# Another written order for the first part of a delta-rule and feed-forward kernel, with eight more loads held behind TensorE

## The chip, the cores and the metric

The kernel runs on one core of a Trainium2 chip. A core has five engines, each working through its own list of instructions in order: TensorE (PE in the profile; its weight loads are shown apart as PEld), VectorE (DVE), ScalarE (ACT), GpSimd (POOL) and SyncE (SP), which here only issues transfers. Engines wait for each other, and for transfers, by semaphores. The metric is the device time of one execution in microseconds (us); less is better.

## What is computed

There are two blocks. The first is a delta-rule attention over 4 batches, 8 heads, 768 tokens and 48 channels: a 48x48 state for each batch and head is read by the query and corrected by the key at every token. The second takes its output, as 3072 rows of 384, through a feed-forward network with 2048 hidden units and the hard-swish function between its two matrix products.

```python
def _attn_ref(q, k, v, beta):
    k_n = k / (np.linalg.norm(k, axis=-1, keepdims=True) + 1e-06)
    ...
    for t in range(S):
        y[:, :, t] = einsum('bhd,bhde->bhe', q[:, :, t], state)
        v_old = einsum('bhde,bhd->bhe', state, kt)
        state = state + bt * einsum('bhd,bhe->bhde', kt, vt - v_old)

def _moe_ref(x, w_in, w_out):
    h = x @ w_in
    g = h * np.clip(h + 3.0, 0.0, 6.0) / 6.0
    return g @ w_out
```

The arrays q, k, v and beta arrive as 32-bit floats; both weight matrices arrive as 64-bit floats and are turned into 32-bit ones on the chip.

## The kernel before, in words

The 768 tokens are cut into 24 chunks t of 32 tokens; 4 batches x 32 tokens fill the 128 partitions. Within a chunk the recurrence becomes a triangular system. Its inverse is made for four chunks at a time on VectorE (`halves_of` for chunks 1 to 4, `inverse` for later ones); chunk 0 alone has its own way, a product of powers on TensorE (`product`). The feed-forward network works on blocks of two chunks.

For the first part of the run, every engine's order of work is written out by hand in the string ORDER. Each word is one step of a Python generator; `do` takes the words one after the other and emits the instructions of that step. `*n` repeats a word. The order in which an engine's instructions are emitted is the order in which it does them, so ORDER fixes all five lists at once. The words, with the generator's step counted from 0 behind a dot or, for loads, a number:

- k, q, v (`load_k`, L168; `load_q`, L180; `load_v`, L193): one load of 48 KB each, four of them (one for each batch) for each chunk; SP issues them. w (`load_w`, L331): one of 16 pieces of raw weights, 768 KB each, also on SP: w0 to w7 are of w_in, w8 to w15 of w_out. B (L1383): one of four loads of beta, issued by ScalarE. In this text k0 to k3 are the four loads of chunk 0's keys, w0 is the first piece of weights, and so on.
- a (`scales`, L356): one of four passes by ScalarE over the exponents of a piece of weights; c (`convert`, L378, L383, L389): one of three steps by VectorE that make 32-bit numbers of it. Piece i is made by a.4i to a.4i+3 and c.3i to c.3i+2; c.3i+2 needs a.4i+3.
- n0, n1, n2, n4 (`norms`): the keys' norms of chunk 0, chunk 1, chunks 2 and 3, chunk 4. For n0, n1, n4: .0 square on ScalarE (L407), .1 sum on VectorE (L413), .2 root on ScalarE (L417), .3 to .6 on VectorE (L420 to L431). n2 has two squares and two sums first.
- p0 to p4 (`prep`): .0 scales a chunk's keys on GpSimd (L510); .1 and .3 transpose keys and queries on TensorE (L524); .2 and .4 copy these to KQ on ScalarE (L532); .5 makes the products sc of keys and queries on TensorE (L547); .6 masks them on VectorE (L558). m (`mask`, L486) and b (`scaled`, L498) are GpSimd's parts of it.
- x0 (`product`): sixteen steps for chunk 0's inverse, by turns on VectorE (L606 to L656), TensorE (L596) and ScalarE (L624, L643).
- z (`settings`, VectorE): z.1 transposes beta to where all others read it (L255), which needs the four loads B; z.2 to z.5 are small constants. s (`more_settings`, GpSimd, L285 and L293): zeros in buffers.
- h0 (`chain` of chunk 0): .0 TensorE pz (L827), .1 ScalarE copy to R (L927), .2 TensorE su (L938), .3 VectorE state (L956). y0 is the rest of the chunk's output.
- i1 (`halves_of`): the inverse of chunks 1 to 4, which needs p1.6 to p4.6: i1.0 is the transpose A (L469), then some thirty small steps on VectorE (L730, L735), then the transpose X (L473); then x1 to x4 (`join`) finish it chunk by chunk on TensorE (L684).
- ua and ub, ra, ga and so on: pieces of the first matrix product (`up`, L994) for block 0, and their evaluation on ScalarE and VectorE; u: pieces of both matrix products for later blocks.

A capital K, Q, V or W is the same load with one more wait: `behind_tensor` makes its issue on SP wait until the last TensorE instruction emitted so far has ended. Before the change there is one such word, for w12.

The trace shows that the eighth load behind a piece of weights is issued only once that piece has landed: w0 is issued at 6.75 us and lands at 12.25, and the eighth load behind it, q4, is issued at 12.27. Where the loads go to buffers that are used again, they wait for the last reader too.

Of the kernel before, what the change touches and what calls it, by code (L numbers as in the profile page):

```python
# [19 lines left out]


ORDER = """
k*2 B*3 k*2 n0 k*2 z B s*2 n0*6 k*2 q*2 n1 q n1 q w k p0 z*3 k n1*2 k*2 n1*2 z p0*2 s k p0*3 a k a
m0 a n2 m1 p0 x0*2 w q x0 n1 x0*3 c*2 n2 a k s p1*2 a s*2 k q s*2 x0 n2 k*2 c x0 n2 x0 w q a*4 q p1
n2 k*2 a x0 m2 p1 c*2 p1 n2*3 b1 q b0 s p1 x0 q w x0 n2 q*2 c*3 x0 n4 k p1 k p2*2 x0*2 a*2 c a*2 q*3
a*2 w v p3*2 q x0 q n4 p2*2 c p2 v c n4*2 a*3 z v n4 c a m3 v c p2 n4*2 q p2 k c b2 h0 c h0 w a*2 h0
p4*2 a*2 m4 p3 q*4 h0 q k w p4*2 c*5 v*2 p3 k p3*3 k*2 p4*2 v*2 p4 m6 k a w a w i1*3 k i1*7 a i1*2 a
i1*2 v i1*2 k b3 k y0 c y0*3 ua*2 ra*2 i1*3 w v ga v a*3 i1*2 ua i1 h1 i1 q w ua ra ua i1 ra*2 ga i1
k ua a*2 ra ga i1 ga ua ra ua ra i1 ga i1*4 ua ga n5 x1*2 k x1 c a ra v a*2 ga x2 k*2 ga*2 ua*2 x1
ra*2 x1*2 ua h1*2 n5 k ga c ra ga*2 h1 c y1*2 ua ra w ga ua ra x2 n5 ga y1*2 ua ra ga h1 v*3 n5*2 k  # L30
y1*2 ua a ra x2 ub*2 a n5 rb*2 h1 x3 ga c*2 v W a h2 y2 gb ub rb gb x2 gb ub*2 n5*2 b4 rb n5 x2*2 h2
gb rb gb m5 a n5*2 ub rb gb v c q*2 v q*5 n5 ub n5 rb gb h2 y2 c h2 q ub y2*2 rb ub p5 b5 h2 rb gb*2
a*2 x3 p5 ub y2*2 k p5*2 h2 rb h3 p5 gb h3 ub*2 q rb gb rb gb ub a x3 p6 v c x4 x3 rb gb ub p7 rb gb
y3 c*2 v c p7*2 y3 v p7*2 b6 x3 q x3 ub h3 a p6*2 c p5*2 rb gb k m7 w p6 h3 u p6 k*2 q*3 a*2 y3 a p6
c y3 v y3*2 u n9 v k q a c a c*2 u*2 ru gu w k a*2 c a*2 x4 c*2 ru p7 a gu k u a*2 p7 p6 m8 u*3 a k
u*2 k h3 w ru*2 a*2 gu*2 x4 c*2 x4 k c*2 a p8 k a*2 u ru k h3 u*2 h4 ru a b8 gu k gu y4 p8*3 u h4
k*2 c q k*9 q u p8*2 k ru k*2 gu k c n9 q u q*2 p8 k*2 b7 n9*2 x4 i2 u x4 q i2*2 q ub ru gu u rb gb
i2*2 h4*2 u*2 i2 ru i2*6 y4 i2 gu i2*7 u i2 ru gu i2 u*3 ru i2*4 gu ru i2*2 v i2 c gu u*3 a u ru c
i2 u*2 i2 gu i2*3 q i2*5 y4 n9 i2 e*2 n9*2 i2*4 q i2 y4 e n9 u ru i2*3 u h4 i2 ru*2 gu h4 u n9 i2*2
u i2 e i2*6 y4 u k n9*3 u gu i2 y4 n9 i2 p9 q i2*2 gu  # L40
"""


# [1507 lines left out]
```

## Time and profile before

| what | value |
|---|---|
| median of three runs | 665.89 us (664.8 to 666.0) |
| the profiled execution's own time | 665.93 us |
| its span | 664.1 us |
| instructions in it | 26330 |
| TensorE matmul, busy | 636.2 us (96% of the span) |
| VectorE, busy | 487.1 us (73%) |
| ScalarE, busy | 272.1 us (41%) |
| GpSimd, busy | 203.5 us (31%) |
| moved by transfers | 33.27 MB, mean 50 GB/s |

The share of each engine is a mean over a short first part, in which the engines wait for one another, and a long second part, in which TensorE is busy nearly without a gap. The profile's slices and its table by stretches tell these parts from one another. In the timeline a row has the start, the length, the engine, the line and the operation with output and input; in square brackets stand the idle time just before it and what ended this. "SPq" rows are the issues of transfers by SP.

### The profile page before, as it was taken

To read this page: it belongs to the slowest core of one execution; us is meant where nothing else is said; L and a number is where in the kernel's file an instruction comes from. 1 tells how busy PE (TensorE), PEld (TensorE's weight loads), DVE (VectorE), ACT (ScalarE), POOL (GpSimd) and SP (SyncE) were. 2 spreads that over 40 slices of the span, in tenths; PEclk is the share of its full clock that TensorE was granted. 3 is DMA by queue.
4 is the path that set the end of the run, shared out by engine and by line. 5 is a ranking of instruction groups with operands and counts; after the bars stand their busy time and mean duration, and the time that the engine had idled before them with its cause. 6 is when DMAs were issued, how large, how long until landed. Compare 5 with 4: busy or idle time off the path is not lost.

```text
span 664.1 us, 26330 instructions
## 1 busy us (share of the span) xinstructions
PE 636.2 (96%) x11544; PEld 568.1 (86%) x11544; DVE 487.1 (73%) x1146; ACT 272.1 (41%) x532; POOL 203.5 (31%) x320
## 2 busy tenths in 40 slices
PE   2769999999999999999999999999999999999997
PEld 1658987776789989989989999999999999999997
DVE  4899867898555697657979748989658998456353
ACT  5897679331233143142144244244244144153350
POOL 6531112003511320562254354064052241331430
PEclk9659999999999999999999999999999999999999
DMA  7897246212140030041030030020020020000000
GB/s 175 206 236 197 76 98 161 49 28 41 23 83 8 10 66 3 2 85 27 2 74 3 2 74 3 3 61 2 3 50 2 2 50 1 23 19 2 25 1 25
DMA packets 88499, 33.27 MB, mean 50 GB/s; under 512 B 80160, under 2 KB 83232, under 8 KB 88384
## 3 DMA queue, kind: packets, MB, share of 16 engines
q1 hardware_dynamic: 88128, 31.29, 20.9%
q8 instruction: 91, 1.49, 0.9%
q10 hardware_dynamic: 256, 0.30, 0.2%
q14 instruction: 24, 0.20, 0.1%
HBM read 26.84 MB, written 4.72 MB: 48 GB/s over the span
## 4 chain that ended last, share of the span: by engine, by line
PE 90%; DVE 3%; DMA 2%; SPq 2%; ACT 1%; issue 1%; POOL 0%; ACTq 0%; DVEq 0%; POOLq 0%
PE po L1218 28%; PE ph L1066 20%; PE ph L994 16%; PE po L1154 6%; PE ks L806 3%; PE pt L524 3%; PE su L938 3%; PE pz L827 3%; PE py L827 3%; PE sc L547 3%; PE yt L873 1%; DMA spare<-in_moe_w_in_dram 1%; PE pi L684 1%; DMA w_out<-in_moe_w_in_dram 1%; SPq L168 1%
## 5 line engine op out<-in xcount | busy, mean ns | idle before, releaser
L1066 PE MATMUL ph<-xT,w_in 128*128 128x128 f32 (+1 forms) x560 | 121.4, 321 | 0.7 <-ACT KQ L532 0.5
L994 PE MATMUL ph<-xT,w_in 128*128 128x256 f32 (+1 forms) x576 | 117.1, 353 | 0.9 <-ACT xT L877 0.6
L1218 PE MATMUL po<-w_out,g 128*128 128x192 f32 x640 | 110.6, 326 | 0.0
L994 PEld LDWEIGHTS ph<-xT,w_in 128*128 128x128 f32 x576 | 95.2, 194 | 13.9 <-ACT xT L877 1.0
L1218 PEld LDWEIGHTS po<-w_out,g 128*128 128x128 f32 x640 | 104.6, 190 | 0.5
L1066 PEld LDWEIGHTS ph<-xT,w_in 128*128 128x128 f32 x560 | 91.1, 191 | 5.9 <-ACT KQ L532 0.7
L1030 POOL TENSOR_TENSOR g<-g 128x256 f32<-128x256 f32 x112 | 67.9, 608 | 83.2 <-ACT g L1080 78.8
L1218 PE MATMUL po<-spare,g 128*128 128x192 f32 x480 | 86.7, 332 | 0.0
L1218 PEld LDWEIGHTS po<-spare,g 128*128 128x128 f32 x480 | 77.2, 190 | 1.8
L1001 ACT ACTIVATE g<-ph,halves 128x256 f32<-128x256 f32 (+1 forms) x96 | 41.0, 436 | 74.2 <-PE ph L994 74.2
L1228 POOL TENSOR_TENSOR o<-o,u 128x192 f32<-128x192 f32 x18 | 13.2, 731 | 175.8 <-ACT o L1225 97.2
L1080 ACT ACTIVATE g<-ph 128x512 f32<-128x512 f32 x56 | 33.4, 597 | 81.8 <-PE ph L1066 81.8
L1204 DVE TENSOR_TENSOR g<-g 128x512 f32<-128x512 f32 x80 | 55.5, 715 | 5.6 <-PE po L1218 5.6
L759 DVE TENSOR_TENSOR pr<-A 128x30 f32<-128x30 f32 (+9 forms) x150 | 57.5, 383 | 2.7
L764 DVE TENSOR_TENSOR A<-A,pr 128x30 f32<-128x30 f32 (+9 forms) x150 | 55.7, 371 | 3.7
L1004 DVE SCALAR_TENSOR_TENSOR g<-g,ph 128x256 f32<-128x256 f32 (+1 forms) x96 | 34.7, 371 | 29.4 <-ACT g L1001 29.0
L356 ACT ACTIVATE spare<-spare,places 128x768 uint16<-128x768 uint16 (+1 forms) x56 | 52.6, 944 | 2.8 <-DMA kf<-in_k_dram 1.7
L1093 DVE TENSOR_TENSOR g<-ph,g 128x256 f32<-128x256 f32 x56 | 23.5, 420 | 38.5 <-PE ph L1066 30.9
L1225 ACT ACTIVATE o<-po 128x192 f32<-128x192 f32 x40 | 13.2, 330 | 83.2 <-PE po L1218 79.6
L1154 PE MATMUL po<-w_out,g 128*128 128x384 f32 x128 | 45.2, 491 | 0.0
L1107 DVE SCALAR_TENSOR_TENSOR g<-o,g 128x512 f32<-128x512 f32 x56 | 40.7, 726 | 5.9 <-ACT o L1104 5.9
L1104 ACT ACTIVATE o<-g,halves 128x512 f32<-128x512 f32 x56 | 40.4, 722 | 8.7 <-DVE g L1107 5.7
(141 smaller groups left out, 989.1 us busy)
## 6 DMA issues: line engine op xcount, KB each, us to landing
kf<-in_k_dram SPq DMA_DIRECT2D x96, 48.0 KB, 2.4
qb<-in_q_dram SPq DMA_DIRECT2D x96, 48.0 KB, 2.8
vf<-in_v_dram SPq DMA_DIRECT2D x96, 48.0 KB, 2.2
out_dram<-o SPq DMA_DIRECT2D x92, 48.0 KB, 1.6
spare<-in_moe_w_in_dram SPq DMA_DIRECT2D x4, 768.0 KB, 5.9
w_out<-in_moe_w_in_dram SPq DMA_DIRECT2D x4, 768.0 KB, 6.0
w_out<-in_moe_w_out_dram SPq DMA_DIRECT2D x4, 768.0 KB, 6.9
spare<-in_moe_w_out_dram SPq DMA_DIRECT2D x4, 768.0 KB, 5.0
```

The costliest lines, as they stand in the source:

```text
L356: nc.scalar.activation(out=z, in_=z if n else d.bitcast(I16)[:, :, :, 3], func=func, bias=places[:, n : n + 1], scale=scale,)
L759: nc.vector.tensor_tensor(out=pv, in0=A[:, j + 1 :, j].unsqueeze(2).to_broadcast([n, w, j]), in1=A[:, j, 0:j].unsqueeze(1).to_broadcast([n ...
L764: nc.vector.tensor_tensor(out=A[:, j + 1 :, 0:j], in0=A[:, j + 1 :, 0:j], in1=pv, op=ALU.subtract)
L994: nc.tensor.matmul(ph[:, cols], lhsT=w_in[:, s, f * 128 : (f + 1) * 128], rhs=xT[:, s, cols], start=(s == 0), stop=(s == NKT - 1),)
L1001: nc.scalar.activation(out=g, in_=ph, func=ACTF.Relu, bias=half, scale=1.0 / 6.0)
L1030: nc.gpsimd.tensor_tensor(out=out, in0=a, in1=b, op=op)
L1066: nc.tensor.matmul(ph[:, n], lhsT=w, rhs=x, start=start, stop=stop, skip_group_check=True)
L1104: nc.scalar.activation(out=r, in_=g, func=ACTF.Relu, bias=half, scale=1.0 / 6.0)
L1107: nc.vector.scalar_tensor_tensor(out=g, in0=r, scalar=1.0, in1=g, op0=ALU.min, op1=ALU.mult)
L1154: nc.tensor.matmul(pos[c][:], lhsT=gs[blk, f // 2][:, f % 2, c * P : (c + 1) * P], rhs=w_out[:, f, :], start=(f == 0), stop=(f == NFC - 1),)
L1204: nc.vector.tensor_tensor(out=A(f, *out, 4), in0=A(f, *a, 4), in1=A(f, *b, 4), op=op)
L1218: nc.tensor.matmul(ps[n][:], lhsT=A(f - f % 2, *a)[:, f % 2], rhs=b[:, f], start=(f == 0), stop=(f == HF - 1),)
```

## The change

Only the string ORDER changes; no function does. It has 782 words before and after. The 622 words that are not loads are the same words, in another order for about the first 120 of them (up to x0.15 and p2.6 in the list above, all well before i1.0); from there on their order is the same, but for two of GpSimd's s words that come later. The 156 loads that SP issues are the same too, but stand in other places over the whole of ORDER. Nine of them are held behind TensorE, where it was one: q11, v2, w6, w10, w11, k35, k37, w12 (as before) and w13.

The first SP loads before are k0 to k7, q0 to q3, w0, k8 to k13, w1; after, they are k0, k1, q0, k2 to k4, q1, q2, w0, k5, q3, k6 to k11, w1. On ScalarE, beta's third and fourth load were issued ahead of and behind n0.0, and are now both behind it. On VectorE, z.1 stood behind n0.6 and now stands ahead of it.

The diff:

```diff
 ORDER = """
-k*2 B*3 k*2 n0 k*2 z B s*2 n0*6 k*2 q*2 n1 q n1 q w k p0 z*3 k n1*2 k*2 n1*2 z p0*2 s k p0*3 a k a
-m0 a n2 m1 p0 x0*2 w q x0 n1 x0*3 c*2 n2 a k s p1*2 a s*2 k q s*2 x0 n2 k*2 c x0 n2 x0 w q a*4 q p1
-n2 k*2 a x0 m2 p1 c*2 p1 n2*3 b1 q b0 s p1 x0 q w x0 n2 q*2 c*3 x0 n4 k p1 k p2*2 x0*2 a*2 c a*2 q*3
-a*2 w v p3*2 q x0 q n4 p2*2 c p2 v c n4*2 a*3 z v n4 c a m3 v c p2 n4*2 q p2 k c b2 h0 c h0 w a*2 h0
-p4*2 a*2 m4 p3 q*4 h0 q k w p4*2 c*5 v*2 p3 k p3*3 k*2 p4*2 v*2 p4 m6 k a w a w i1*3 k i1*7 a i1*2 a
-i1*2 v i1*2 k b3 k y0 c y0*3 ua*2 ra*2 i1*3 w v ga v a*3 i1*2 ua i1 h1 i1 q w ua ra ua i1 ra*2 ga i1
-k ua a*2 ra ga i1 ga ua ra ua ra i1 ga i1*4 ua ga n5 x1*2 k x1 c a ra v a*2 ga x2 k*2 ga*2 ua*2 x1
-ra*2 x1*2 ua h1*2 n5 k ga c ra ga*2 h1 c y1*2 ua ra w ga ua ra x2 n5 ga y1*2 ua ra ga h1 v*3 n5*2 k
-y1*2 ua a ra x2 ub*2 a n5 rb*2 h1 x3 ga c*2 v W a h2 y2 gb ub rb gb x2 gb ub*2 n5*2 b4 rb n5 x2*2 h2
-gb rb gb m5 a n5*2 ub rb gb v c q*2 v q*5 n5 ub n5 rb gb h2 y2 c h2 q ub y2*2 rb ub p5 b5 h2 rb gb*2
-a*2 x3 p5 ub y2*2 k p5*2 h2 rb h3 p5 gb h3 ub*2 q rb gb rb gb ub a x3 p6 v c x4 x3 rb gb ub p7 rb gb
-y3 c*2 v c p7*2 y3 v p7*2 b6 x3 q x3 ub h3 a p6*2 c p5*2 rb gb k m7 w p6 h3 u p6 k*2 q*3 a*2 y3 a p6
-c y3 v y3*2 u n9 v k q a c a c*2 u*2 ru gu w k a*2 c a*2 x4 c*2 ru p7 a gu k u a*2 p7 p6 m8 u*3 a k
-u*2 k h3 w ru*2 a*2 gu*2 x4 c*2 x4 k c*2 a p8 k a*2 u ru k h3 u*2 h4 ru a b8 gu k gu y4 p8*3 u h4
-k*2 c q k*9 q u p8*2 k ru k*2 gu k c n9 q u q*2 p8 k*2 b7 n9*2 x4 i2 u x4 q i2*2 q ub ru gu u rb gb
-i2*2 h4*2 u*2 i2 ru i2*6 y4 i2 gu i2*7 u i2 ru gu i2 u*3 ru i2*4 gu ru i2*2 v i2 c gu u*3 a u ru c
-i2 u*2 i2 gu i2*3 q i2*5 y4 n9 i2 e*2 n9*2 i2*4 q i2 y4 e n9 u ru i2*3 u h4 i2 ru*2 gu h4 u n9 i2*2
-u i2 e i2*6 y4 u k n9*3 u gu i2 y4 n9 i2 p9 q i2*2 gu
+k*2 q B k s B k*2 z n0 q*2 B*2 n0 w k n0 q n0 s k n0*2 k*4 z k n1 n0 z p0*2 n1 p0 c w z k*2 n1 q z
+p0 q p0 a k m0 n1 q k q n1 a s a n1 w n2 s n1 p0 c a p0 x0 k x0 p1 q p1 x0*2 p1 s k n2 m2 n2 x0 b0 k
+x0 v a b1 k*2 n2*2 p1 x0 c x0 c*2 a*2 k p1 x0 a x0 n4 n2 w q s k a*2 c n2*3 a p1 q m1 Q p2*2 c a c q
+x0 w v q n4 x0 a c*2 q p1 x0 p3 V s n4*2 a p3 x0 v w q c a p2 a x0 a q a p2*2 a z n4 q c a q m3 c p2
+q n4*2 W x0 p2 c b2 v h0 v c h0 a*2 h0 q p4*2 a*2 m4 p3 h0 p4*2 c*4 v c q p3*4 p4*3 k m6 a k a i1*5
+k i1*3 w i1*2 a i1 q i1 w a i1*3 k i1 b3 y0 c v y0*3 k ua q ua k ra*2 i1*2 w i1 ga a v a*2 i1 s i1
+ua i1 h1 i1 ua v ra k ua i1 ra*2 ga i1 ua a*2 ra ga i1 W ga ua ra ua ra i1 ga i1*4 ua ga n5 x1*2 v
+x1 c a ra a*2 ga W x2 ga*2 ua*2 v x1 ra*2 x1*2 ua h1*2 n5 ga c ra ga*2 h1 c y1 k v y1 ua ra ga ua k
+ra k x2 n5 ga v y1*2 ua ra q ga h1 n5*2 y1*2 ua a k ra x2 ub*2 a n5 k rb*2 K h1 x3 ga c q c W a h2 q
+y2 gb ub rb gb x2 gb k ub*2 n5 K n5 b4 rb n5 x2 q x2 h2 gb rb gb m5 a n5*2 ub q s rb gb c n5 q ub k
+n5 v rb gb h2 y2 c h2 ub y2*2 rb ub p5 q v*2 b5 h2 rb gb*2 k*2 a*2 x3 p5 ub q v y2 q y2 p5*2 h2 rb
+h3 v p5 gb h3 ub*2 rb gb rb gb ub a x3 q p6 v c x4 x3 rb gb ub p7 rb gb y3 k c*3 p7 v p7 y3 p7*2 b6
+x3 q x3 q k ub h3 a p6*2 c p5*2 v rb gb m7 p6 h3 u p6 a*2 k y3 a p6 c y3*2 W y3 u n9 a c a c*2 q u*2
+ru gu a*2 c a*2 x4 q k c*2 ru p7 a gu k u q a w a p7 k p6 q m8 u*3 a k u*2 h3 ru*2 a k a k gu*2 x4
+c*2 v x4 k*2 w c*2 a p8 a*2 u ru h3 k u q u h4 ru a b8 gu*2 y4 k p8*2 v p8 k*2 u h4 c u k p8*2 ru gu
+c q n9 u p8 b7 q n9*2 x4 i2 u x4 i2*2 ub ru gu q u q k rb gb i2*2 k h4*2 u*2 i2 ru q k i2*5 k*2 i2
+y4 i2 gu i2*7 k u i2 ru gu i2 u*3 ru i2*4 gu ru i2*3 c gu u q u*2 a u ru c k i2 u*2 i2 gu i2*8 y4 n9
+i2 e k e n9*2 i2*5 y4 e n9 k u ru i2*3 u q h4 i2 ru*2 gu k h4 u n9 i2*2 u i2 e i2*6 y4 u n9*3 u gu k
+i2 y4 n9 i2 p9 i2*2 gu
 """
```

## The prediction

> **What bounds the kernel now.** The table by stretches comes first, since TensorE's 96% is a mean of two unlike parts (columns: stretch, its length, busy time and count for PE, PEld, DVE, ACT and POOL, granted clock, transfer share, GB/s).
>
> ```profile
> 5.00:10.00 5.00, 1.93 (x8) 1.57 (x8) 4.00 (x17) 2.02 (x5) 3.11 (x7) 1.00 0.70 155
> 10.00:15.00 5.00, 1.97 (x129) 1.58 (x128) 2.29 (x7) 3.20 (x4) 1.87 (x5) 1.00 1.13 293
> 20.00:25.00 5.00, 2.73 (x115) 2.16 (x103) 3.79 (x9) 4.93 (x9) 0.00 (x0) 0.50 0.91 216
> 40.00:45.00 5.00, 4.31 (x102) 3.82 (x108) 4.68 (x7) 4.68 (x7) 0.29 (x1) 0.50 0.78 129
> 65.00:70.00 5.00, 5.00 (x155) 4.61 (x155) 3.89 (x12) 2.91 (x8) 0.00 (x0) 1.00 0.14 26
> ```
>
> From 65 us on TensorE has no gap worth naming, and its words there are in the same order after the change. So what the change is worth is how much earlier or later TensorE becomes full. Until 47 us it is not TensorE that is short, but ScalarE and VectorE, near 4.7 of 5 us busy from 25 us on. The chain of waits, in order of time, says what follows:
>
> ```profile
> 46.77 1.87 DVE A L469
> ...
> 57.77 1.99 DVE X L473
> 59.76 0.12 DVE g L1004
> 59.88 0.37 DVE sums_in L694
> 60.29 0.73 PE pi L684 x54
> ```
>
> From 46.7 us (i1.0) to 60.3 us the chain is VectorE's work on the inverse of chunks 1 to 4; its words are the same in both orders, and TensorE waited 1.0 us ahead of L684 at 60.29. A shift of i1.0 is therefore a shift of the end, one for one. What brings i1.0 about is read from the timeline:
>
> ```profile
> 6.75 0.45 SPq L331 DMA_DIRECT2D spare<-in_moe_w_in_dram  x1
> 7.18 0.83 POOL L510 TENSOR_TENSOR kb<-kf,inv 128x384 f32<-128x384 f32 x1 [1.89 <-DVE inv L431]
> 10.24 0.45 SPq L331 DMA_DIRECT2D spare<-in_moe_w_in_dram  x1
> 12.27 0.31 SPq L180 DMA_DIRECT2D qb<-in_q_dram  x1
> 12.33 2.92 ACT L356 ACTIVATE spare<-spare,places 128x768 uint16<-128x768 int16 x3 [1.66 <-DMA kf<-in_k_dram]
> 18.80 0.52 ACT L407 ACTIVATE sq<-kf 128x384 f32<-128x384 f32 x1 [1.16 <-DVE ss L413]
> 33.13 0.60 ACT L532 ACTIVATE KQ<-pt 128x512 f32<-128x512 f32 x1 [1.38 <-PE pt L524]
> 37.62 0.47 ACT L927 ACTIVATE R<-pz 128x384 f32<-128x384 f32 x1
> 39.74 1.21 DVE L956 TENSOR_TENSOR state<-state,su 128x384 f32<-128x384 f32 x2
> 43.15 1.09 ACT L532 ACTIVATE KQ<-pt 128x512 f32<-128x512 f32 x2 [0.28 <-PE pt L524]
> ```
>
> ScalarE's first conversion pass, a.0, starts at 12.33; its last copy ahead of i1, p4.4, ends at 44.24. In these 31.9 us it waited 1.16, 1.38 and 0.28 us, 2.8 in all, so it worked 29.1 us. Its words between a.0 and p4.4 are the same set after the change: 24 passes (0.93 us each in a row), 8 copies (0.52), squares, roots, x0.3, x0.10, h0.1. It is the engine to follow.
>
> One more thing is needed, how loads fare behind a piece of weights. The transfers' view of 0 to 4.6 us, and then of 8.2 to 8.7 us (loads issued behind w0):
>
> ```profile
> kf<-in_k_dram SPq DMA_DIRECT2D x8, 48.0 KB, 2.1
> ```
> ```profile
> kf<-in_k_dram SPq DMA_DIRECT2D x2, 48.0 KB, 5.1
> ```
>
> A small load behind w0 takes 5.1 us to land, not 2.1: it gets through only after w0 (issued 6.75, landed 12.25; q4, the eighth load behind it, goes at 12.27). The six loads behind w0 then come some 0.3 us apart.
>
> **The change, part by part.** Nothing is added but eight waits on SP; all else moves.
>
> *The start.* k3 is SP's fifth issue, not its fourth: one issue takes 0.49 us, so n0.0 goes from 4.78 to 5.27. B2 and B3 stand behind n0.0 on ScalarE: issued about 5.3 and 5.6 to 5.9, landed by about 7.6 with the 1.85 us that the chain shows for beta. z.1 (0.97 us) stands ahead of n0.6 and waits for them: n0.5 ends at 7.36 (6.86 + 0.49), z.1 runs 7.6 to 8.6, n0.6 to 8.8, and the first keys (L510) start at 8.85, not 7.18. TensorE's first transposes run 9.75 to 10.85.
>
> w0 goes at 0.80 + 8 x 0.49 = 4.7, not 6.75, and lands at 10.2. But k5, q3, k6 and k7 are now behind it: at 0.3 us apart, k7 lands at 11.5. n1.0 needs k7, and on ScalarE p0.2 stands behind n1.0. So ScalarE, which before went on at 6.42, sits until 11.5; then n1.0 (0.5), p0.2 (0.5), n1.2 behind VectorE's n1.1 (to 13.0) and p0.4: a.0 starts at 13.45, +1.1. Were k7 not held by w0, p0.2 would go at 10.9 and a.0 at 12.3, +0.0.
>
> What this buys: on VectorE, c.0, z.2 to z.4 and c.1 (0.55 + 1.0 + 1.0 us) fall into time in which it idles anyway (2.29 of 5 busy at 10 to 15).
>
> *ScalarE's waits from a.0 on.* Each by adding rows in the new order. (1) TensorE's p0.5 runs 13.65 to 14.85; c.1 holds VectorE to 15.25, then p0.6 and x0.0 to 16.95; x0.1 ends 17.8, p1.1 at 18.9. ScalarE has done a.3 at 17.55 and stands at x0.3 and p1.2: 0.35 + 0.85 = 1.2 us. (2) The places of w1, w2, w3 are each the ninth behind the one before, so each goes just after the former has landed: 10.7, 16.9, 23.0, where it was 10.24, 15.12, 19.59. w3 lands at 28.5 to 29.8 (5.5 to 6.8 us, the rows' ends); ScalarE comes to a.12 at 28.9. 0 to 0.9, I take 0.2, from the median of 5.7 to 6.0. (3) q11 is held behind p1.5; behind q11 wait q12, w4 and all else on SP. p1.5 needs x0.9 on TensorE, this needs x0.8 (VectorE, to 25.15): p1.5 ends at 27.5. w4 goes at 28.5 (26.45 before; 26.0 without the hold) and lands, with 5.1 to 6.8 us, at 33.6 to 35.3. ScalarE is at a.16 at 33.5. 0 to 1.8; I take 0.5, by w0's 5.5 us, since little else moves then. (4) p2.4 has moved behind a.17: it ends at 13.45 + 21.1 us of work + 1.2 + 0.7 = 36.4. Then sc (1.2), pz (1.5) and their gaps (0.2) must run before h0.1, at 39.3; a.18 and a.19 cover 1.9 of it, the wait is 1.0. Before, p2.4 stood ahead of a.16 and h0.1 did not wait (37.62). Sum 2.9, against 2.8 before: these hardly differ, they only stand elsewhere.
>
> *From h0.1 on.* h0.1 is at 39.3, 1.7 us late; su and the state follow as before (2.12 us from L927 to L956), then c.15 to c.19, p3.6, p4.6 as before (6.95 us): i1.0 at 48.4, +1.7. p4.4 ends at 13.45 + 29.1 + 2.9 = 45.5 by ScalarE's own sum, + 0.3 for the transposes, + 2.45 as before: 48.2. The two agree; I take +1.6. v2 is held behind x0.12 (to 31.5), so w5 goes at 32.5 (32.37 before), lands behind w4 at 38.5 and is needed at 39.7: nothing, but no more than 1 us of cover. w6, held behind p2.5, goes at 37.9, lands at 43.5, c.18 is due at 44.5: nothing, with 1 us of cover.
>
> *GpSimd and the rest.* m0 to m4, b and s move by less than GpSimd's waits of 4 to 13 us there. TensorE's part before 47 us moves beside these waits. Nothing.
>
> *After i1.* w10 and w11 go behind pieces of ua, needed 20 us later. k35 goes behind ub and is needed two or three steps later by n5.6 (74.75 us): up to 0.5 us of ScalarE, which has gaps of 0.3 to 1.3 us there: nothing on TensorE. k39 was behind w13, and n9's square waited 1.25 us for it at 99.28; now it is early: TensorE's 0.2 us gap at 99 goes. w13 is held behind y3.2 (97.4 us, 92.22 before), lands at 103, is due (a.52) at 103.3; w15 goes at 108, lands at 113.5, due at 113.2: 0 to 0.5 us of ScalarE, which TensorE felt as a sixth of it at 99. Sum -0.2.
>
> **The sum**: +1.6 - 0.2 = +1.4 us on the profiled execution's 665.93, whose span is 664.1; it lies 0.04 us above the median, so 667.3 us, 0.2% more.
>
> The beta loads go on ScalarE's queue while w0 is in flight on SP's. No row shows this (B3 went 2 us ahead of w0 before): between 7.4 (1.85 us, no delay) and 10.2 (not before w0 has landed); I take 7.6, since their rows had 1.85 us with eight key loads in flight. [...]
>
> **Rivals.**
> *VectorE is the bound* (faster). At 25 to 46 us it is as busy as ScalarE, and the new order gives it 1.5 us (c.0, c.1) of that stretch's work in time it idled. If ScalarE's copies keep ahead, i1.0 comes 1.5 us earlier: 665.9 - 1.5 - 0.2 = 664.2. It decides if a.0 starts by 12.5 and the waits (1) to (4) stay under 1.2 us in all. For it: the 25 to 45 us stretches. Against: k7 behind w0, and h0.1's one us.
> *The start costs nothing* (same). k7 and B3 get through, a.0 at 12.3, the rest as I sum it: 1.6 - 1.1 - 0.2: 666.2.
> *The queue is worse* (slower). B3 lands with w0 at 10.2: keys at 12.3, p0.4 at 15, a.0 1.6 us later than in my sum; or w4 at its late end (1.3 more): 668.6 to 669.
>
> **How the numbers follow.** A measurement here tells 0.2% (1.3 us) from no change: same is 664.6 to 667.2. My forecast (0.38) is at this edge, by its terms 666.6 (w3, w4 in time) to 668.5 (both late); I put 0.25 of it above and 0.13 below. VectorE as the bound 0.20, the start costs nothing 0.22 (0.03 of it below 664.6), the worse queue 0.20. Slower 0.25 + 0.20 = 0.45; same 0.13 + 0.19 = 0.32; faster 0.23. The range is 664.0 to 669.0: it leaves out part of the first and last rival.
>
> **What the profile after would show.** Right: L510's first row near 8.9, n1.0 released by a transfer near 11.5, a.0 near 13.4, waits of about a microsecond at h0.1 and near 18 us, w4 issued near 28.5, L469 near 48.3, no gap at 99. Wrong: a.0 at 12.3 or earlier; L469 ahead of 46.7; a wait on w5, w6, w13 or w15, for which I saw cover of a microsecond or less.

## The result, and the profile after

The changed kernel takes 671.75 us (median of four runs, 671.09 to 673.67), the kernel before 665.35 in the runs beside it: a ratio of 1.0084, with a 95% interval of 1.0062 to 1.0106. It is slower by some 5.6 us by this ratio (the medians lie 6.4 apart), where 1.4 was forecast. The profiled execution took 671.67 us with a span of 669.9; before these were 665.93 and 664.1, so the span grew by 5.8. Line numbers after are one higher than before (L469 is now L470).

The chain of waits of the kernel after comes first. Its columns are start, length and what the time went to; "issue" is time for which the profile shows no wait.

```profile
5.29 6.76 issue
12.08 0.84 POOL kb L511
...
27.56 0.38 PE sc L548 x13
27.94 1.59 issue
29.54 1.08 PE sc L548 x51
30.63 0.31 SPq L181
30.99 1.51 SPq L181
32.55 5.84 DMA w_out<-in_moe_w_in_dram
38.47 1.00 ACT spare L357
...
52.37 1.86 DVE A L470
...
63.29 1.98 DVE X L474
```

Nearly the whole loss can be read here. Nothing the chain can follow happens from 5.29 to 12.08; then the keys are scaled (L511, 7.18 before). Later the chain does something that it did not do before: it goes through SyncE. The products sc of chunk 1 (p1.5) are broken in two by 1.59 us; when their second part is done, SP can issue q11 (L181, held behind them), then q12, then w4 at 32.55; ScalarE's pass a.16 starts when w4 has landed, at 38.47. i1.0 (L470) follows at 52.28 by the timeline, 5.59 us later than the 46.69 of before, and the transpose X at 63.29 instead of 57.77, 5.52 later. The span grew by 5.8. The row of i1.0 in the timeline before:

```profile
46.69 1.94 DVE L469 STREAM_TRANSPOSE A<-L 128x1024 f32<-128x1024 f32 x1
```

The timeline of the kernel after says what stood in for the "issue" of the chain's first line.

```profile
4.66 0.45 SPq L332 DMA_DIRECT2D spare<-in_moe_w_in_dram  x1
5.03 0.63 ACTq L1384 DMA_DIRECT2D spare<-in_beta_dram  x2
...
10.93 0.98 DVE L256 STREAM_TRANSPOSE beta_tok<-spare 128x768 f32<-128x768 f32 x1 [3.84 <-DMA kf<-in_k_dram]
11.66 0.52 ACT L408 ACTIVATE sq<-kf 128x384 f32<-128x384 f32 x1 [5.21 <-DMA kf<-in_k_dram]
...
12.08 0.83 POOL L511 TENSOR_TENSOR kb<-kf,inv 128x384 f32<-128x384 f32 x1 [6.79 <-DVE inv L432]
15.46 2.94 ACT L357 ACTIVATE spare<-spare,places 128x768 uint16<-128x768 int16 x3
38.47 0.99 ACT L357 ACTIVATE spare<-w_out,places 128x768 uint16<-128x768 int16 x1 [3.94 <-DMA w_out<-in_moe_w_in_dram]
43.65 0.49 ACT L928 ACTIVATE R<-pz 128x384 f32<-128x384 f32 x1 [0.95 <-PE pz L828]
52.28 1.94 DVE L470 STREAM_TRANSPOSE A<-L 128x1024 f32<-128x1024 f32 x1
```

Beta's last two loads are issued from 5.03 on, 0.4 us after w0. The transpose of beta (z.1, L256) stands ahead of n0.6 on VectorE and runs at 10.93. n0.6, the keys, TensorE's first transposes and ScalarE's copies all follow it; ScalarE reaches a.0 at 15.46 (12.33 before) and then waits 3.94 us for w4. The releaser named at L256 is a load of keys; the experiments show that what L256 waits for is beta. (A second profile of the same kernel, further down, names beta itself.)

Two stretches of each part, in the table whose columns the prediction gives:

```profile
5.00:10.00 5.00, 0.00 (x0) 0.00 (x0) 1.09 (x4) 0.82 (x2) 0.29 (x2) 1.00 0.97 221
10.00:15.00 5.00, 1.97 (x8) 1.57 (x8) 2.69 (x12) 1.34 (x4) 2.92 (x4) 1.00 0.68 156
75.00:80.00 5.00, 4.42 (x150) 4.02 (x149) 4.32 (x10) 4.44 (x9) 0.00 (x0) 1.00 0.08 17
85.00:90.00 5.00, 4.51 (x151) 4.01 (x150) 4.45 (x13) 2.58 (x5) 3.15 (x5) 1.00 0.55 89
```

From 5 to 10 us TensorE does nothing at all, and VectorE works 1.09 us of 5 where it worked 4.00. The lower two rows are new too: where before each five microseconds from 65 to 95 us were full, TensorE now lacks 0.58 and 0.49 us. The rows of TensorE's timeline in which it waited for nothing that the profile shows:

```profile
24.17 0.64 PE L597 MATMUL pi<-sums_in 32*32 32x32 f32 x51 [0.54 <-issue]
29.54 1.06 PE L548 MATMUL sc<-KQ 64*32 64x64 f32 x51 [1.59 <-issue]
77.82 0.72 PE L995 MATMUL ph<-xT,w_in 128*128 128x128 f32 x5 [0.58 <-issue]
86.56 0.67 PE L828 MATMUL py<-R,LB 32*32 32x48 f32 x42 [0.49 <-issue]
```

Each stands in the middle of a run of equal matmuls (13 of sc, then 51; 22 of py, then 42). Before there were two such places in the first 130 us, 0.50 us and 0.20:

```profile
39.91 0.45 PE L938 MATMUL su<-R,sums_in 32*64 32x48 f32 x3 [0.50 <-issue]
99.44 2.32 PE L994 MATMUL ph<-xT,w_in 128*128 128x256 f32 x10 [0.20 <-issue]
```

The account in the two profiles: X is 5.52 later; TensorE loses 1.07 in the two gaps after it; the 0.20 at 99 us are gone; from 300 to 500 us TensorE is busy 199.74 us instead of 199.26, 0.48 more. 5.52 + 1.07 - 0.20 - 0.48 = 5.9, and the span grew by 5.8.

### The profile page after: what moved, and what is told of

It reads as the page before. It is cut to its first block, busy times and chain, and to the rows that moved or that the text cites. A ratio compares the mean times of both kernels' runs of the same rounds, so it can differ in the third digit from the quotient of the medians.

```text
span 669.9 us, 26329 instructions
## 1 busy us (share of the span) xinstructions
PE 635.8 (95%) x11544; PEld 568.2 (85%) x11544; DVE 485.8 (73%) x1146; ACT 272.4 (41%) x532; POOL 202.8 (30%) x320
## 3 DMA queue, kind: packets, MB, share of 16 engines
q8 instruction: 91, 1.49, 0.9%
## 4 chain that ended last, share of the span: by engine, by line
PE 92%; DVE 3%; issue 2%; ACT 1%; DMA 1%; POOL 1%; SPq 0%; POOLq 0%; DVEq 0%; ACTq 0%
PE po L1219 28%; PE ph L1067 21%; PE ph L995 15%; PE po L1155 6%; PE ks L807 4%; PE sc L548 3%; PE pt L525 3%; PE pz L828 3%; PE py L828 3%; PE su L939 3%; PE yt L874 1%; DMA w_out<-in_moe_w_in_dram 1%; ACT spare L357 1%; PE pi L685 1%; PE pi L597 1%
## 5 line engine op out<-in xcount | busy, mean ns | idle before, releaser
L1031 POOL TENSOR_TENSOR g<-g 128x256 f32<-128x256 f32 x112 | 68.2, 610 | 82.5 <-ACT g L1081 78.1
L511 POOL TENSOR_TENSOR kb<-kf,inv 128x384 f32<-128x384 f32 x24 | 21.9, 915 | 78.5 <-issue 44.0
```

The source lines that it names most:

```text
L1031: nc.gpsimd.tensor_tensor(out=out, in0=a, in1=b, op=op)
```

## The experiments

The question was which of the moves brings the 5 to 6 us: the order of the words, the loads at the start (beta, w0), the holds, or the loads after i1. Each time is a median, its ratio is to the kernel before on the same chip (667.62 us for the first four, 667.36 for the next four, 668.28 for the last four). Single executions of one kernel lay 2 to 9 us apart on these chips (the kernel before: 665.7 to 674.0 in the last group), so readings rest on ratios with their intervals and on places inside a profile. Runs built from the kernel before keep its line numbers (L469 is i1.0 there).

### The hold of q11 taken away

```diff
-x0 v a b1 k*2 n2*2 p1 x0 c x0 c*2 a*2 k p1 x0 a x0 n4 n2 w q s k a*2 c n2*3 a p1 q m1 Q p2*2 c a c q
+x0 v a b1 k*2 n2*2 p1 x0 c x0 c*2 a*2 k p1 x0 a x0 n4 n2 w q s k a*2 c n2*3 a p1 q m1 q p2*2 c a c q
```

> The changed kernel with one letter changed: q11 is an ordinary load again (v2 and the others stay held). Theory A (the hold on q11 keeps w4, and this keeps ScalarE, which waited 3.9 us for w4 at 38.47): w4 goes near 27 us instead of 32.55 and lands near 33, the wait at a.16 is gone; about 1 us comes back as a wait at h0.1; L470 near 49 instead of 52.28, time about 668.5 (3 us less than 671.75). Theory B (the new order of the other words is at fault, with the hold only showing where it waits): the wait moves to p2.4 or h0.1, L470 stays above 51.5 and the time above 671.

Measured: 671.52 us, ratio 1.0062 (1.0045 to 1.0080). The wait did go: w4 is issued at 26.64, not 32.55, and ScalarE doesn't wait at a.16. But i1.0 came only from 52.28 to 50.31. What took the place of the wait is in TensorE's timeline of this kernel:

```profile
29.89 1.06 PE L548 MATMUL sc<-KQ 64*32 64x64 f32 x51 [2.14 <-issue]
39.87 0.27 PE L548 MATMUL sc<-KQ 64*32 64x64 f32 x2 [1.87 <-issue]
```

With 1.08 at 24.52 and 1.06 at 43.77, TensorE now stands 6.15 us in such gaps before i1, against 2.13 with the hold, and the copy h0.1 waits 2.13 us for TensorE. So without the hold i1.0 came 2 us earlier in this profile. What that is worth in time can't be told, since the interval lies over that of the changed kernel (1.0062 to 1.0106); it isn't the main loss.

### Beta ahead of the norms

```diff
-k*2 q B k s B k*2 z n0 q*2 B*2 n0 w k n0 q n0 s k n0*2 k*4 z k n1 n0 z p0*2 n1 p0 c w z k*2 n1 q z
+k*2 q B k s B*3 k*2 z n0 q*2 n0 w k n0 q n0 s k n0*2 k*4 z k n1 n0 z p0*2 n1 p0 c w z k*2 n1 q z p0
...
```

> The changed kernel with beta's third and fourth load issued right behind the second, ahead of n0.0 and of w0; nothing else. Theory A (these two land only with w0, and z.1, which stands ahead of n0.6, waits for them): z.1 starts at 7.4 instead of 10.93 and the first keys (L511) at 8.6 instead of 12.08; n1.0 still waits for k7 until 11.7; a.0 near 13.5 instead of 15.46, the rest shifts with it, w4 too: about 669.8, 2 us less. Theory B (beta's lateness costs nothing, since n1.0 stands on k7 anyway): a.0 stays within 0.5 us of 15.46, time 671.5 to 672.

Measured: 668.21 us, ratio 1.0002 (0.9984 to 1.0020). All that moved is beta's third and fourth load on ScalarE's queue, from behind n0.0 to ahead of it; every hold and every load of SP stands as in the changed kernel. The timeline:

```profile
7.98 0.98 DVE L256 STREAM_TRANSPOSE beta_tok<-spare 128x768 f32<-128x768 f32 x1
...
11.26 0.52 ACT L408 ACTIVATE sq<-kf 128x384 f32<-128x384 f32 x1 [3.94 <-DMA kf<-in_k_dram]
13.09 2.93 ACT L357 ACTIVATE spare<-spare,places 128x768 uint16<-128x768 int16 x3
34.22 0.99 ACT L357 ACTIVATE spare<-w_out,places 128x768 uint16<-128x768 int16 x1 [2.10 <-DMA w_out<-in_moe_w_in_dram]
39.40 0.49 ACT L928 ACTIVATE R<-pz 128x384 f32<-128x384 f32 x1 [0.94 <-PE pz L828]
47.64 1.94 DVE L470 STREAM_TRANSPOSE A<-L 128x1024 f32<-128x1024 f32 x1
```

z.1 comes 2.95 us earlier, a.0 2.37, w4's issue 3.99 (28.56), i1.0 4.64. Two loads of 24 KB decide nearly the whole result.

### The first piece of weights behind the keys

```diff
-k*2 q B k s B k*2 z n0 q*2 B*2 n0 w k n0 q n0 s k n0*2 k*4 z k n1 n0 z p0*2 n1 p0 c w z k*2 n1 q z
+k*2 q B k s B k*2 z n0 q*2 B*2 n0 k n0 q n0 s k n0*2 k w k*3 z k n1 n0 z p0*2 n1 p0 c w z k*2 n1 q z
```

> The changed kernel with w0 issued behind k7 instead of ahead of k5; beta's loads stay behind n0.0. Theory A (it is w0 in front that makes both k7 and beta late, across the two queues): n1.0 near 9 us, z.1 near 7.5 us, first keys near 8.8, a.0 near 12.5 (w0 lands near 12): L470 about 3 us earlier than 52.28, time about 668.7. Theory B (beta is late for a reason of its own, such as its own queue on ScalarE): z.1 stays near 10.9, keys near 12, a.0 near 14.5, time near 670.8.

Measured: 667.98 us, ratio 1.0012 (0.9994 to 1.0030). Here beta stays where the change put it, and is issued at 5.03 as there, but w0 goes at 6.65 instead of 4.66. The timeline:

```profile
7.81 0.98 DVE L256 STREAM_TRANSPOSE beta_tok<-spare 128x768 f32<-128x768 f32 x1 [0.72 <-DMA spare<-in_beta_dram]
...
8.77 0.52 ACT L408 ACTIVATE sq<-kf 128x384 f32<-128x384 f32 x1 [2.31 <-DMA kf<-in_k_dram]
```

The transpose now starts at 7.81, and the releaser is beta by name; a.0 follows at 12.91 and i1.0 at 47.44. Since only w0 moved, it was w0 that held beta, although the two are on different queues. How it did so is told by the transfers' view, taken by single microseconds (q10 is ScalarE's queue; the columns are packets, MB and the share of the transfer engines' time). With w0 behind, from 6 to 7 us:

```profile
q10 hardware_dynamic: 32, 0.05, 14.6%
```

All 32 packets of the two loads move within one microsecond. In the kernel after, from 7 to 8, 8 to 9 and 9 to 10 us:

```profile
q10 hardware_dynamic: 16, 0.02, 6.5%
...
q10 hardware_dynamic: 11, 0.02, 5.3%
...
q10 hardware_dynamic: 5, 0.01, 2.7%
```

The same 32 packets, issued at the same time, start a microsecond later and are spread over 2.6 us (7.1 to 9.7), and z.1 starts 1.3 us behind the last. With w0 behind all ran between 6 and 7 us, and z.1 started at 7.81, so at least 0.8 us behind the last.

### Both, and both with fewer holds

Beta early, w0 behind k7, and q11 and v2 not held:

```diff
-k*2 q B k s B k*2 z n0 q*2 B*2 n0 w k n0 q n0 s k n0*2 k*4 z k n1 n0 z p0*2 n1 p0 c w z k*2 n1 q z
+k*2 q B k s B*3 k*2 z n0 q*2 n0 k n0 q n0 s k n0*2 k w k*3 z k n1 n0 z p0*2 n1 p0 c w z k*2 n1 q z
...
-x0 w v q n4 x0 a c*2 q p1 x0 p3 V s n4*2 a p3 x0 v w q c a p2 a x0 a q a p2*2 a z n4 q c a q m3 c p2
+x0 w v q n4 x0 a c*2 q p1 x0 p3 v s n4*2 a p3 x0 v w q c a p2 a x0 a q a p2*2 a z n4 q c a q m3 c p2
...
```

> The three edits together: w0 behind k7, beta's loads all ahead of n0.0, q11 and v2 not held; the changed order of all other words stays. Theory A (start and w4 are all of it): a.0 near 12.3, no wait at a.16, waits of about 1 us at 18 us and at h0.1; L470 at 46 to 47, as before the change (46.69): time 665 to 666.5. Theory B (the order of the other words costs by itself): L470 above 48, time above 667.

Measured: 670.08 us (667.22 to 672.09), ratio 1.0039 (1.0020 to 1.0059). Its profile is of its fastest execution, 667.22, with a.0 at 12.63 and i1.0 at 47.18; w4 goes at 26.27, and a.16 still waits 1.38. Next the same two moves with the holds kept:

```diff
-k*2 q B k s B k*2 z n0 q*2 B*2 n0 w k n0 q n0 s k n0*2 k*4 z k n1 n0 z p0*2 n1 p0 c w z k*2 n1 q z
+k*2 q B k s B*3 k*2 z n0 q*2 n0 k n0 q n0 s k n0*2 k w k*3 z k n1 n0 z p0*2 n1 p0 c w z k*2 n1 q z
```

> The changed kernel with the start mended (w0 behind k7, beta's loads ahead of n0.0) and all nine holds kept: against the run that also freed q11 and v2, this tells what these holds cost. Theory A (they only keep w4 back): w4 goes 1 to 2 us later than the 26.27 of that run, ScalarE waits 2 to 3 us at a.16 instead of 1.4, L470 near 48.5, ratio 1.004 or more. Theory C (they keep big loads away from TensorE's own instruction fetch, whose delays show as gaps inside a row of equal matmuls with no wait behind them): L470 within 0.5 us of 47.2, fewer such gaps, and a ratio below 1.002, with a smaller spread of the times than 667.2 to 672.1.

Measured: 669.67 us (667.89 to 673.68), ratio 1.0029 (1.0005 to 1.0052); a.0 at 12.84, but a wait of 1.46 us for w4 at 34.67 and one of 1.42 us for TensorE at h0.1 (40.33), and i1.0 at 48.78. Neither theory holds as it stands: w4 goes at 26.69, only 0.4 us later than without the holds, and the ratio lies between the two. What the holds of q11 and v2 cost once the start is mended can't be told from these two intervals. The two mends do not add: each alone puts a.0 at 13, and together they bring it 0.1 to 0.3 us further, while w4 lands later than ScalarE is ready. A third form also put z.1 back behind n0.6:

```diff
-k*2 q B k s B*3 k*2 z n0 q*2 n0 k n0 q n0 s k n0*2 k w k*3 z k n1 n0 z p0*2 n1 p0 c w z k*2 n1 q z
+k*2 q B k s B*3 k*2 z n0 q*2 n0 k n0 q n0 s k n0*2 k w k*4 n1 n0 z*2 p0*2 n1 p0 c w z k*2 n1 q z p0
...
```

> The changed kernel with the start mended as above and z.1 put back behind n0.6. If z.1 is on the path of the first keys: L511 near 8.0 instead of 9.1, and a.0 near 12.2 (then w0's landing sets it, not the copies) instead of 12.6; L470 0.4 to 1 us earlier than with the start mended alone, ratio 0.001 less. If ScalarE stands on something later anyway: no difference in L470 beyond 0.2 us.

Measured: 669.63 us, ratio 1.0039 (1.0013 to 1.0065). The keys come at 8.13 instead of about 9, but a.0 only at 12.97, since the constants that a.0 reads are then made later on VectorE. i1.0 is at 48.27. Once beta is there in time, the ratios show no worth in z.1's place.

### The words without the loads, and the loads without the words

The new order of the words up to i1.0 with the loads where they were before, no new hold, and before's list behind i1.0:

```diff
-k*2 B*3 k*2 n0 k*2 z B s*2 n0*6 k*2 q*2 n1 q n1 q w k p0 z*3 k n1*2 k*2 n1*2 z p0*2 s k p0*3 a k a
+k*3 B k s B*2 k*2 z n0 k*2 B n0 q*2 n0 q n0 s q n0*2 w k*3 z k n1 n0 z p0*2 n1 p0 c k z k w n1 q z
...
```

> Only the order of the words that are not loads is the new one, up to i1.0; the loads go out in the sequence and with the holds of the kernel before, and all from i1.0 on is the kernel before. Theory A (the places of the loads are the whole loss): L470 between 45.7 and 47.7 (46.69 before), ratio 0.998 to 1.002. Theory B (the new order of the words loses by itself): L470 at 49 or later, ratio 1.004 or more.

Measured: 671.14 us (667.21 to 675.56), ratio 1.0042 (1.0019 to 1.0065). The start is good (keys at 8.31, a.0 at 12.80). The loss is in TensorE's gaps between 38 and 50 us; two rows of the timeline:

```profile
38.23 0.37 PE L547 MATMUL sc<-KQ 64*32 64x64 f32 x2 [1.52 <-issue]
40.10 0.49 ACT L927 ACTIVATE R<-pz 128x384 f32<-128x384 f32 x1 [2.81 <-PE pz L827]
```

The gap hits p2.5, which the new order has placed shortly ahead of h0; ScalarE's copy h0.1 waits 2.81 us behind it, and i1.0 is at 50.62. Two more gaps, 1.17 us at 43.08 and 0.49 at 49.30, follow. So in this profile the order of the words has a price of its own, by where the gaps fall in it. The other half, the new loads and holds with the words of before:

```diff
-k*2 q B k s B k*2 z n0 q*2 B*2 n0 w k n0 q n0 s k n0*2 k*4 z k n1 n0 z p0*2 n1 p0 c w z k*2 n1 q z
+k*2 B*2 q k*2 n0 B k z B s*2 n0*6 q*2 w k q k*2 n1*2 k p0 z*3 k n1*2 k*2 n1*2 z p0*2 s w p0*3 a k a
...
```

> The other half: the words that are not loads stay in the order of the kernel before up to i1.0, but the loads go out in the new sequence with the new holds, and all from i1.0 on is the changed kernel. Theory A: n1.0 waits for k7 until 11.5, but z.1 stands behind n0.6 here, so the first keys go near 7.4; a.0 near 13.5 (12.33 before), w4 later than 28 with a wait of 1 to 3 us at a.16; L470 at 48.5 to 51; ratio 1.003 to 1.007. Theory B (only together with the new words do the loads lose): L470 below 47.7, ratio below 1.002.

Measured: 678.87 us, ratio 1.0180 (1.0145 to 1.0216). That is more than either theory had. a.0 is at 15.60: the first keys go early, at 7.56, but the constants that a.0 reads stand behind n1's steps on VectorE, and these behind k7. w4 is issued only at 36.40. The timeline:

```profile
39.46 0.60 ACT L532 ACTIVATE KQ<-pt 128x512 f32<-128x512 f32 x1 [4.26 <-PE pt L524]
42.49 1.00 ACT L356 ACTIVATE spare<-w_out,places 128x768 uint16<-128x768 int16 x1 [2.24 <-DMA w_out<-in_moe_w_in_dram]
```

i1.0 is at 57.36. The holds and places made for the new order of words are worse with the old one; and neither half alone, nor both, beats the kernel before.

### The list behind i1.0

The changed kernel once more, as the partner of the next two (no edit):

> The changed kernel once more, on the chip and beside the runs of the other experiments, so that ratios can be set side by side. All theories: a ratio between 1.006 and 1.010, L470 at 51 to 53.

Measured: 673.89 us, ratio 1.0092 (1.0059 to 1.0124): the loss is there again, on the chip of the last four. In this profile L256 names what it waits for:

```profile
11.25 0.98 DVE L256 STREAM_TRANSPOSE beta_tok<-spare 128x768 f32<-128x768 f32 x1 [3.73 <-DMA spare<-in_beta_dram]
```

i1.0 is at 52.41, against 52.28 in the first profile, but the span is 673.6 against 669.9. So between these two the places up to i1.0 agree better than the spans do. Then its first part with before's list behind i1.0, so that all loads and holds there are before's:

```diff
-q n4*2 W x0 p2 c b2 v h0 v c h0 a*2 h0 q p4*2 a*2 m4 p3 h0 p4*2 c*4 v c q p3*4 p4*3 k m6 a k a i1*5
+q n4*2 W x0 p2 c b2 v h0 v c h0 a*2 h0 q p4*2 a*2 m4 p3 h0 p4*2 c*4 v c q p3*4 p4*3 k m6 a k a q k*2
...
```

> The first part of the changed kernel up to i1.0, loads and all; from i1.0 on the kernel before (four loads of k and q, one of v, w7, w8 and two s words that this had sent by then go out just ahead of i1.0). Theory A (besides the start and w4, the places and holds of the later loads cost TensorE about a microsecond at 65 to 95 us, as gaps inside py and ph rows): L470 near 52.3 as in the changed kernel, TensorE's gaps of 0.5 us at 77 and 86 us gone, ratio 0.0015 below that of the changed kernel run again. Theory B (all of it is made before i1.0): the same ratio within 0.0005.

Measured: 673.45 us, ratio 1.0079 (1.0050 to 1.0108). In the two profiles the gaps of TensorE from 65 to 95 us are 0.97 and 1.35 in the first and 0.16 in the second, and the spans are 673.6 and 671.5; but the medians differ by 0.44 us, with intervals that lie over each other. The same part with beta early as well:

```diff
-k*2 q B k s B k*2 z n0 q*2 B*2 n0 w k n0 q n0 s k n0*2 k*4 z k n1 n0 z p0*2 n1 p0 c w z k*2 n1 q z
+k*2 q B k s B*3 k*2 z n0 q*2 n0 w k n0 q n0 s k n0*2 k*4 z k n1 n0 z p0*2 n1 p0 c w z k*2 n1 q z
...
```

> As the run before this one, and with beta's loads ahead of n0.0 and w0. If beta's place and the later loads are the two largest terms: L470 near 47.7, as with beta's loads alone, TensorE full from 66 to 90 us, ratio 0.999 to 1.001. If the later loads cost nothing: 1.001 to 1.003.

Measured: 668.63 us, ratio 1.0009 (0.9987 to 1.0031), against 1.0002 for beta early with the new list behind i1.0 (on another chip). On the chip of the last four, beta's place alone took 1.0079 to 1.0009. The list behind i1.0 makes no difference that these runs can tell from none, in either pair.

### Four more pieces of weights in flight

The gaps of TensorE without a wait had no cause yet. To the kernel before were added four loads of 768 KB, w11's data sent again to the same buffer; its words were left alone.

```diff
+        elif word == "D":
+            nc.sync.dma_start(
+                out=raws[11].rearrange("p s f z -> p s (f z)"), in_=weights[11][1].bitcast(U32)
+            )
-ra*2 x1*2 ua h1*2 n5 k ga c ra ga*2 h1 c y1*2 ua ra w ga ua ra x2 n5 ga y1*2 ua ra ga h1 v*3 n5*2 k
+ra*2 x1*2 ua h1*2 n5 k ga c ra ga*2 h1 c y1*2 ua ra w D ga ua ra x2 n5 ga y1*2 ua ra ga h1 v*3 D
...
```

> The kernel before with w11 sent four more times, one behind the other, between about 57 and 85 us, to where it lies anyway: nobody waits for these copies but the next one. In that stretch TensorE is full in the kernel before (25.00 of 25 us). Theory C (big loads in flight delay TensorE's instruction fetch): gaps of 0.3 to 2 us without a wait behind them appear inside rows of equal matmuls at 60 to 90 us, at the places where a packet of the instruction queue is due, TensorE 1 to 3 us short of full there, ratio 1.0015 to 1.005. Rival (TensorE's gaps in the changed kernel are made by its own words and waits): no such gap, ratio 0.9995 to 1.001; small loads behind the copies may be late, which would show as a wait on a transfer at ScalarE.

Measured: 672.62 us, ratio 1.0070 (1.0045 to 1.0094). The copies are issued at 64.06, 68.81, 76.59 and 83.94 us. TensorE, which in the profile of before was busy 34.80 of the 35 us from 65 to 100, is busy 30.05 here; the two rows of the table by stretches, before and with the copies:

```profile
65.00:100.00 35.00, 34.80 (x1120) 30.57 (x1121) 27.43 (x68) 25.50 (x53) 5.90 (x8) 1.00 0.36 86
65.00:100.00 35.00, 30.05 (x978) 26.92 (x976) 25.50 (x64) 20.40 (x45) 5.11 (x8) 1.00 0.55 147
```

Its timeline:

```profile
70.73 0.74 PE L938 MATMUL su<-R,bkb 32*64 32x48 f32 x47 [0.85 <-issue]
75.38 0.71 PE L994 MATMUL ph<-xT,w_in 128*128 128x128 f32 x4 [1.02 <-issue]
84.85 0.65 PE L827 MATMUL py<-R,LB 32*32 32x48 f32 x41 [1.23 <-issue]
90.52 0.38 PE L524 MATMUL pt<-ident,qb 128*128 128x128 f32 x2 [1.54 <-issue]
```

With 0.32 at 98.85 these are 4.96 us, and for none of them does the profile show a wait for data. So loads that nobody waits for slow TensorE, some 1.2 us for each 768 KB here. (X was also 1.5 us later than in the profile of before, ahead of the first added load; 1.5 + 4.75 is about the span's 6.4.)

## Why the prediction was wrong, step by step

**Beta's landing is the step that failed.** The sum had B3 landed at 7.6, between ends of 7.4 and 10.2. Measured: z.1 at 10.93, 3.3 us later than the value taken and beyond the upper end. From there the keys are at 12.08 (8.85 forecast) and a.0 at 15.46 (13.45). The 7.6 were taken from rows in which beta had only key loads beside it, and so did not bear on a load issued 0.4 us behind 768 KB; w0 on one queue and beta on another were costed as if they shared nothing. The rival "the queue is worse" had the place right, keys at 12.3, with a chance of 0.20, and priced it at 668.6 to 669, where the range ended. It added 1.6 us for beta or 1.3 for a late w4; both came, and TensorE's gaps besides.

The packets of beta did go between those of w0: from 7 to 8 us 16 of them moved, and on SP's queue 167 (0.34 MB), so beta did not stand behind the whole of w0. But they went slowly: 32 packets took 2.6 us where they took under 1 with w0 behind. From the last packet to z.1 it was 1.3 us, against at least 0.8 with w0 behind, so at most 0.5 us of the delay lies there.

**The second term that was mis-sized is w4.** The hold of q11 behind p1.5 was seen and its order on SP was right; w4 was forecast at 28.5 and a wait of 0 to 1.8 us, 0.5 taken. Measured: w4 at 32.55, a wait of 3.94. SP's own waits from 24 to 34 us in the kernel after:

```profile
SPq L181 <- PE sc L548: 5.9, 1, 5.9
```

The hold turned a late start into a late load. Against the run with beta early, a.0 is 2.37 us later, p1.5 has a gap of 1.59 in its middle, and w4 goes 3.99 later: each went one for one into w4. With beta mended, w4 is issued at 28.56, as forecast, but by luck: p1.5 ended a microsecond earlier than the sum had it (26.5 for 27.5), and q11 and q12 kept SP for 2.1 us behind it, where 1.0 was allowed. And still a.16 waits 2.10, more than the 1.8 of the late end: ScalarE was there earlier than the sum had it (32.1, not 33.5).

**What the sum had no term for: TensorE's gaps.** The two after i1 are 1.07 us, the two before it 2.13. The two before i1 come with the late start: all four profiles of the new order of words in which beta is late have a gap at these same two places, 221 and 349 matmuls in (0.5 to 1.1 us and 1.6 to 2.3), and of the seven in which beta is in time, six have none at either, and one has 0.29 us at the first. So a start 2.4 us late at a.0 became 4.6 at i1.0. The profile of before showed two of these, 0.50 and 0.20, and the prediction read the second as ScalarE's wait on n9. The forecast for the list behind i1.0 was -0.2; what was measured there can't be told from nothing, the gap at 99 us did go, and others came.

**What was right.** k7 behind w0: n1.0 at 11.5 forecast, 11.66 measured. The places of w1, w2, w3, each the ninth load behind the piece before it: 10.7, 16.9, 23.0 forecast, 11.60, 17.14, 22.51 measured. h0.1's wait of 1.0 was 0.95. The wait near 18 us was smaller, 0.63 at 20.69 for 1.2. The pieces w5, w6 and w13 kept their cover, and w15 cost ScalarE 0.33 us (0 to 0.5 forecast). And i1.0 does carry the end: 5.59 there, 5.8 in the span. The kernel with beta early is the case that the sum described, and its places come near: a.0 13.09 (13.45), w4 28.56 (28.5), h0.1 39.40 (39.3), i1.0 47.64 (48.3, +1.6; measured +0.95). Part of this is luck, since the longer wait at a.16 and ScalarE's earlier arrival there cancel. The ratio of 1.0002 (0.9984 to 1.0020) is -1.1 to +1.3 us, so the forecast of +1.4 us lies just above what was measured for a kernel in which beta was not late.

**The other rivals.** VectorE as the bound (faster) needed a.0 by 12.5 and under 1.2 us of waits; a.0 came at 15.46. No run with the new order met these conditions: with the words alone a.0 was at 12.80, but h0.1 waited 2.81 us. So this rival is not refuted as such; no run's ratio is below 1. "The start costs nothing" needed k7 and B3 to get through behind w0; neither did.

What stays open: why the mended kernels, with a.0 earlier still, are not better than beta early alone; their executions spread over 5 to 9 us, and only one of each was seen in a profile. It also was not tried whether beta on a third queue would pass w0.

## What to carry to other kernels

A small load that starts the critical path should be issued ahead of a large one, also when the large one is on another queue: issuing two loads of 24 KB 0.4 us behind one of 768 KB made 3 us at their reader and, through what followed, 5 us at the end. A load held behind an engine ties the queue to that engine's delays, so price the hold with the engine late, not on time: here a start 2.37 us later and p1.5's gap of 1.59 us came back in w4 one for one, as 3.99 us. When moving large loads into a stretch in which TensorE is full, count them as a cost even if nobody waits for them (here four of 768 KB took 4.75 us of TensorE from 65 to 100 us), and look in its timeline for idle time with no releaser in the middle of equal matmuls.

## What the runs showed that was not expected

Everything that the traces show of TensorE's unexplained gaps fits waits for its own instructions; this is a reading of their places, and no run changed the transfer of instructions itself. The transfers' view has a queue of kind "instruction", q8, with 91 packets and 1.49 MB in the whole run, 16 KB a packet; the profile's page counts 11544 matmuls and 11544 weight loads, so a packet would be 23088 / 91 = 254 of TensorE's instructions, by an estimate that takes all of q8 to be TensorE's. Three things tie the gaps to it. By the counts of the table by stretches, the matmuls before a gap are 221 and 349 in the kernel after (128 apart, that is 256 instructions with the weight loads), and 1366, 1494, 1749 and 1875 with the four more loads (128, 255 and 126 apart). The gaps after i1 in the kernel after stand at 1493 and 1748, so within one matmul of two of those, though 1.7 to 2.4 us later and in another kernel. And TensorE goes on 2.3 to 2.7 us behind the start of a q8 packet each time: packets at 21.5, 27.1, 75.5 and 83.9 us, ends of the gaps at 24.17, 29.54, 77.82 and 86.56; with the four more loads, packets at 68.2, 73.0, 82.4 and 88.0, ends at 70.73, 75.38, 84.85 and 90.52. That more loads make these gaps is shown by the last experiment.

Which step is late can be read where a gap marks the end of a block, as the instructions of one such packet are called here. In these two kernels the next packet starts 1.0 to 1.2 us behind that end when no gap follows (29.54 to 30.70, 77.82 to 78.86, 86.56 to 87.67; with the four more loads 75.38 to 76.48, 90.52 to 91.59), and 2.3 to 3.1 us behind it when one follows (24.17 to 27.06; 70.73 to 73.00, 84.85 to 87.96). The packets themselves take 1.0 to 1.2 us ahead of these gaps and 0.9 to 1.5 without one. So the packet starts late; it does not move more slowly. Between the block's end and the late packet's start 0.8 to 0.9 MB of other loads moved, and 0.1 MB or less in the prompt cases. What holds the packet back beyond that is not shown, and ahead of the 0.58 us at 77.82 no piece of weights was moving.

Not every packet of q8 comes with a gap. From 130 to 300 us the queue has 21 packets in the kernel after, and TensorE is busy 170.00 of the 170 us. In the first 100 us it has 17, and there a gap at a block's end took up to 2.3 us in these profiles.

The gaps also say why one mend bought so little: taking the hold of q11 away saved ScalarE's 3.94 us of waiting and gave 4.0 us more of gaps. For the kernels with the start mended this is not shown.
